# An attention and mixture-of-experts kernel: q's low halves subtracted on all 128 rows, without the two copies across partitions

## The chip, the cores and the metric

The kernel runs on one core of a Trainium2 chip. The metric is the device time of one execution in microseconds. The core has five engines with a queue each: TensorE (PE, its weight loads shown apart as PEld), VectorE (DVE), ScalarE (ACT), GpSimd (POOL) and SyncE (SP, which only issues transfers). POOL issues transfers too: the indirect ones, whose rows are picked by a table.

## What is computed

Three layers in a row, on float32 inputs:

```
scores = q @ k^T / 8                       # 4 batches x 8 heads, 768 tokens, 64 per head
keep only the first n_sink keys and a window of `window` keys behind each query
a = softmax(scores);  x = a @ v            # x: 3072 tokens x 512
h = x @ w_in;  x = (h - tanh(h)) @ w_out   # 512 -> 2048 -> 512
logits = x @ w_gate + modality_bias[modality_id];  e = argmax(logits)
out = softmax(logits)[e] * (relu(x @ w1[e]) @ w2[e])     # 8 experts, 512 -> 1024 -> 512
```

The scores decide, through everything behind them, which expert a token goes to, so most products are made from two terms: each float32 operand is split into a high half, which is the operand rounded to the type that the matmul reads (fp32r), and a low half, which is the rest.

## The kernel before

**Staging.** The 3072 tokens go through attention and the second layer in 12 chunks of 256 (index `c`). Attention works on 96 units `U`, one head of one chunk each, eight to a chunk, and runs about a chunk ahead of the second layer. In the second layer a chunk has 16 steps `f`: `L1` makes `h` (line 172), `gact` bends it on ACT, DVE and POOL, `g_split` splits the result into high and low halves (the low one on POOL, line 216), and `L2` adds it up in `acc` (line 246). After a chunk, `r_route` picks the experts of its tokens on DVE and writes a list of slots to DRAM (`xs`) with two indirect transfers from POOL (line 656). Behind the last chunks the expert layer runs, with its own lines from 712 on.

**A unit of attention.** `a_load` and `a_loadv` load q, k and v, laid out so that q and k stand twice, on rows 0 to 63 and again on rows 64 to 127 (64 is the size of a head). The first 14 units use them as they are. From unit 14 on, `a_split` makes three tiles: `K` with k's high half on the upper 64 rows and its low half on the lower 64; `A`, cast from q on all 128 rows by ACT (line 211), its lower 64 rows then overwritten by q's low half on POOL (line 216); and `B`, the same two halves the other way round, brought there by two transfers of SP (lines 301 and 302). `a_S` multiplies both with `K` (lines 314 and 315). As the contraction runs over 128 rows, A with K gives high by high and low by low, and B with K gives the two cross terms: all four products. `a_splitv` splits v in the same way (line 216 again, tile `V`). Then come the softmax, the transposes (347, 348), the band selection on POOL (355, tile `X`) and the product with v (413 to 419).

**Order.** A table of times `self.o` sets when each step is written out; the instructions then stand in that order in each engine's queue, and each engine works through its queue in order. A framework puts in the waits: each engine counts its finished instructions in a semaphore (`PE_49`, `Activation_49`, `Pool_49`, `DVE_49`), and each transfer counts its landing in one of eight semaphores for SP's transfers (`DMAHW0_49` to `DMAHW7_49`) or for POOL's (`DMASW0_49` to `DMASW7_49`). Tiles `A`, `B`, `K` and the raw `q`, `k`, `v` have two buffers each.

Of the kernel before, what the change touches and what calls it, by code (L numbers as in the profile page):

```python
# [17 lines left out]
B, H, S, D = 4, 8, 768, 64  # L18
# [18 lines left out]
def f32(ap):  # L37
    return ap.bitcast(F32)


class Kern:
# [250 lines left out]
    def a_split(self, U):  # L292
        nc = self.nc
        u, p = self.u[U], self.spp
        q, k = u.pop("q"), u.pop("k")
        A = p.tile([P, CH], F32R, tag="A", name=f"A{U}")
        Bt = p.tile([P, CH], F32R, tag="B", name=f"B{U}")
        K = p.tile([P, KW], F32R, tag="K", name=f"K{U}")
        self.cast(self.e("qhi", U < 16), A, q)
        self.sub(self.e("qlo", U < 16), A[D:], q[D:], f32(A[D:]))  # L300
        nc.sync.dma_start(f32(Bt[:D]), f32(A[D:]))
        nc.sync.dma_start(f32(Bt[D:]), f32(A[:D]))
        self.cast(self.e("khi", U < 16), K, k)
        self.sub(self.e("klo", U < 16), K[D:], k[D:], f32(K[D:]))
        u.update(A=A, B=Bt, K=K)
# [698 lines left out]
```

## Time and profile before

| | |
|---|---|
| median of 3 runs | 1222.81 us (1222.67 to 1223.86) |
| the profiled execution | 1225.8 us, of which the span from first to last instruction is 1224.0 us |
| PE busy | 1135.9 us, 93% of the span |
| DVE, ACT, POOL busy | 885.5 (72%), 757.4 (62%), 657.7 us (54%) |
| B's transfers | 164 of 64 KB (both sides counted), 2.1 us to landing |
| xs's transfers | 24, on POOL's queue, 3.8 to 7.6 us to landing, median 4.7 |

The stages, read from the trace: up to about 90 us the second layer's weights come in and are decoded; from 190 to 850 us stand the ten stretches in which a chunk's attention and second layer run side by side; from about 860 us on the expert layer runs. A busy PE doesn't say that it runs at its full clock: PEclk is the share of it that was granted, 1.00 or 0.50. An idle stretch of an engine is put down to what the engine waited for last; where several semaphores are waited for, that name can be the wrong one.

### The profile page before, as it was taken

To read this page: it belongs to the slowest core of one execution; us is meant where nothing else is said; L and a number is where in the kernel's file an instruction comes from. 1 tells how busy PE (TensorE), PEld (TensorE's weight loads), DVE (VectorE), ACT (ScalarE), POOL (GpSimd) and SP (SyncE) were. 2 spreads that over 40 slices of the span, in tenths; PEclk is the share of its full clock that TensorE was granted. 3 is DMA by queue.
4 is the path that set the end of the run, shared out by engine and by line. 5 is a ranking of instruction groups with operands and counts; after the bars stand their busy time and mean duration, and the time that the engine had idled before them with its cause. 6 is when DMAs were issued, how large, how long until landed. Compare 5 with 4: busy or idle time off the path is not lost. (4 is left out here: it accounts for less than half of the span.)

```text
span 1224.0 us, 23714 instructions
## 1 busy us (share of the span) xinstructions
PE 1135.9 (93%) x7171; PEld 994.8 (81%) x7171; DVE 885.5 (72%) x2419; ACT 757.4 (62%) x2123; POOL 657.7 (54%) x973
## 2 busy tenths in 40 slices
PE   7879998999899899999899999999798999999993
PEld 3447787988789789989789988988687989999992
DVE  6889896888778687978778887966647566666720
ACT  3445765777577678767577877775726555555620
POOL 4987865777667668767667767763302211211200
PEclk9859998999999899999999999999998999999997
DMA  7654232333323233333333323200909777777500
GB/s 206 203 187 137 75 91 62 102 80 102 60 76 90 71 88 85 98 69 104 60 91 83 104 66 87 81 12 19 343 19 327 238 226 213 222 241 219 168 26 6
DMA packets 88256, 147.98 MB, mean 121 GB/s; under 512 B 18864, under 2 KB 64432, under 8 KB 88112
## 3 DMA queue, kind: packets, MB, share of 16 engines
q1 hardware_dynamic: 83184, 133.16, 37.2%
q0 software_dynamic: 4928, 13.14, 3.0%
q8 instruction: 61, 1.00, 0.4%
q14 instruction: 83, 0.68, 0.2%
HBM read 122.86 MB, written 13.17 MB: 111 GB/s over the span
## 5 line engine op out<-in xcount | busy, mean ns | idle before, releaser
L172 PE MATMUL h<-xt,wi 128*128 128x256 f32 x2304 | 356.1, 290 | 9.9 <-DVE gz L188 9.0
L246 PE MATMUL acc<-wo,g 128*128 128x512 f32 x1152 | 334.5, 407 | 24.0 <-POOL g L216 23.1
L172 PEld LDWEIGHTS h<-xt,wi 128*128 128x128 f32 x2304 | 320.5, 194 | 40.4 <-DVE gz L188 12.4
L246 PEld LDWEIGHTS acc<-wo,g 128*128 128x128 f32 x1152 | 198.6, 192 | 53.1 <-POOL g L216 26.0
L216 POOL TENSOR_TENSOR g<-gz,g 128x256 fp32r<-128x256 f32 x192 | 153.4, 802 | 82.3 <-ACT g L211 78.4
L735 DVE TENSOR_TENSOR ml<-mr,mh 128x1024 fp32r<-128x1024 f32 x104 | 127.9, 1236 | 53.4 <-ACT mh L734 51.8
L778 PE MATMUL mh<-mxt,mh 128*128 128x256 f32 x832 | 157.9, 286 | 3.2 <-DVE mxt L768 2.5
L795 PE MATMUL macc<-mh,mg 128*128 128x512 f32 x416 | 147.9, 401 | 4.3 <-DVE mg L782 4.3
L778 PEld LDWEIGHTS mh<-mxt,mh 128*128 128x128 f32 x832 | 138.1, 193 | 12.1 <-DVE mxt L768 2.9
L189 ACT ACTIVATE u<-u,kt 128x256 f32<-128x256 f32 x192 | 97.8, 509 | 80.2 <-DVE gz L188 73.8
L355 POOL TENSOR_SCALAR_AFFINE_SELECT X<-fl 128x512 fp32r<-128x512 f32 (+1 forms) x192 | 119.2, 643 | 33.6 <-DVE fl L385 24.5
L804 POOL DMA_INDIRECT out_dram<-mo,mi x26 | 28.5, 1096 | 200.2 <-ACT mo L803 196.0
L734 ACT CAST mh<-mr 128x1024 fp32r<-128x1024 f32 x104 | 108.6, 1052 | 40.9 <-PE macc L795 25.2
L188 DVE TENSOR_TENSOR gz<-u,h 128x256 f32<-128x256 f32 x192 | 78.9, 414 | 57.5 <-POOL g L216 34.2
L778 PE MATMUL mh<-mxt,ml 128*128 128x256 f32 x416 | 118.5, 286 | 0.0
L194 DVE SCALAR_TENSOR_TENSOR gz<-gy,gz 128x256 f32<-128x256 f32 x192 | 108.3, 570 | 9.2 <-ACT gy L185 2.7
L328 ACT ACTIVATE e<-e,nm 128x160 f32<-128x160 f32 x192 | 82.0, 427 | 48.0 <-DVE nm L326 46.5
L211 ACT CAST g<-gz 128x256 fp32r<-128x256 f32 x192 | 77.0, 402 | 44.4 <-DVE gz L194 29.7
L337 POOL TENSOR_SCALAR e<-e,sm 128x160 f32<-128x160 f32 x192 | 96.9, 515 | 11.6 <-DVE sm L332 9.6
L216 POOL TENSOR_TENSOR A<-q,A 64x256 fp32r<-64x256 f32 x82 | 69.4, 846 | 56.3 <-issue 14.0
L781 ACT ACTIVATE mg<-mh 128x256 fp32r<-128x256 f32 x104 | 40.3, 387 | 94.2 <-PE mh L778 88.3
L185 ACT ACTIVATE gy<-u,k 128x256 f32<-128x256 f32 x192 | 96.5, 510 | 2.5
(211 smaller groups left out, 2270.5 us busy)
## 6 DMA issues: line engine op xcount, KB each, us to landing
mr<-in_moe_w_dram SPq DMA_DIRECT2D x104, 512.0 KB, 4.7
k<-in_k_dram SPq DMA_DIRECT2D x82, 224.0 KB, 2.7
v<-in_v_dram SPq DMA_DIRECT2D x96, 128.0 KB, 2.3
q<-in_q_dram SPq DMA_DIRECT2D x82, 128.0 KB, 2.2
B<-A SPq DMA_DIRECT2D x164, 64.0 KB, 2.1
rawi<-in_moe_w_in_dram SPq DMA_DIRECT2D x16, 512.0 KB, 5.7
rawo<-in_moe_w_out_dram SPq DMA_DIRECT2D x16, 512.0 KB, 5.6
x2d<-x SPq DMA_DIRECT2D x24, 256.0 KB, 2.2
```

The lines of the kernel that those rows point to most:

```text
L172: nc.tensor.matmul(h[:, :CH], w[:, wl, k * P:(k + 1) * P], x[:, xl, k], start=(n == 0), stop=(n == 11))
L185: nc.scalar.activation(y, u, AF.Square, bias=self.k0, scale=K1)
L189: nc.scalar.activation(u, u, AF.Relu, bias=self.kt, accum_out=self.over[:, n:n + 1])
L194: nc.vector.scalar_tensor_tensor(out=z, in0=y, scalar=KC, in1=z, op0=ALU.add, op1=ALU.mult)
L216: (self.nc.vector if eng == "v" else self.nc.gpsimd).tensor_tensor(out=out, in0=a, in1=b, op=ALU.subtract)
L246: nc.tensor.matmul(o, g[:, gl, t * P:(t + 1) * P], w[:, wl], start=(f == 0 and n == 0), stop=(f == NF - 1 and n == 2))
L337: self.nc.gpsimd.tensor_scalar(out=e, in0=e, scalar1=r, scalar2=1.0, op0=ALU.mult, op1=ALU.mult)
L355: self.nc.gpsimd.affine_select(out=out, in_=in_, pattern=[[0, n], [s, P]], base=0, channel_multiplier=-s, compare_op=ALU.is_gt if prev els ...
L734: nc.scalar.copy(hi, r)
L735: nc.vector.tensor_sub(lo, r, f32(hi))
L778: nc.tensor.matmul(h, w[:, k * P:(k + 1) * P], x[:, xl, k], start=(n == 0), stop=(n == 11))
L795: nc.tensor.matmul(self.macc[g][t], gt[:, gl, t * P:(t + 1) * P], w[:, DM:], start=(f == 0 and n == 0), stop=(f == n8 - 1 and n == 2))
```

## The change

```diff
         self.cast(self.e("qhi", U < 16), A, q)
-        self.sub(self.e("qlo", U < 16), A[D:], q[D:], f32(A[D:]))
-        nc.sync.dma_start(f32(Bt[:D]), f32(A[D:]))
-        nc.sync.dma_start(f32(Bt[D:]), f32(A[:D]))
+        self.sub(self.e("qlo", U < 16), Bt, q, f32(A))
         self.cast(self.e("khi", U < 16), K, k)
```

`A` now keeps q's high half on all 128 rows, and `B` is q's low half on all 128 rows, made on POOL from `q` and `A`. With `K` unchanged, A by K gives high by high and high by low, B by K gives low by high and low by low: the same four products, summed in another order. It touches the 82 units from 14 on. PE, DVE and ACT have the same instructions in the same order as before. POOL has the same number in the same order, with 82 of them on 128 rows instead of 64, and SP loses 164 transfers. The waits that the framework puts in are others.

On POOL, from the indirect transfers of the first chunk's routing on, before (`xs` is the list of slots, `A23` the tile A of unit 23, `V20` the split v of unit 20, `g1_7` the split of chunk 1, step 7; in brackets the semaphores waited for):

```order
L656 DMA xs_63<-pl_336,sl0_2220 4864x2 [waits DVE_49]
L656 DMA xs_63<-pl_336,sl0_2220 4864x2
L216 TENSOR_TENSOR A23_2479<-q23_2164,A23_2479 64x256 [waits DMAHW0_49,DMASW1_49,DMAHW1_49,DMASW0_49,DMAHW3_49,Activation_49,Pool_49]
L216 TENSOR_TENSOR V20_2346<-v20_2161,V20_2346 128x4x64 [waits PE_49,DMAHW4_49,Activation_49,Pool_49]
L216 TENSOR_TENSOR g1_7_2435<-gz1_7_2431,g1_7_2435 128x256 [waits Activation_49]
L355 AFFINE_SELECT X_173<-fl20_2382 128x512 [waits DVE_49]
L355 AFFINE_SELECT X_173<-fl20_2382 128x512
```

The same place on POOL now (line numbers behind the edit are two lower):

```order
L654 DMA xs_63<-pl_336,sl0_2206 4864x2 [waits DVE_49]
L654 DMA xs_63<-pl_336,sl0_2206 4864x2
L216 TENSOR_TENSOR B23_2462<-q23_2150,A23_2461 128x256 [waits DMAHW2_49,PE_49,Activation_49]
L216 TENSOR_TENSOR V20_2330<-v20_2147,V20_2330 128x4x64 [waits DMAHW4_49,PE_49,Activation_49]
L216 TENSOR_TENSOR g1_7_2417<-gz1_7_2413,g1_7_2417 128x256 [waits Activation_49]
L353 AFFINE_SELECT X_173<-fl20_2364 128x512 [waits DVE_49,Pool_49]
L353 AFFINE_SELECT X_173<-fl20_2364 128x512 [waits Pool_49]
```

No instruction moved there; the subtraction's list of waits is shorter by both DMASW semaphores, by two DMAHW ones and by POOL's own, and PE's is new in it, while the two selections now wait for POOL's own semaphore. Before, ten of the 82 subtractions wait for DMASW semaphores, one behind each of the first ten chunks' routing; now none does.

On SP, the transfers around unit 23 and 24, before:

```order
L302 DMA B23_2480<-A23_2479 64x256 [waits DMAHW2_49,DMAHW3_49,PE_49,Activation_49]
L270 DMA k25_2476<-in_k_dram 128x448 [waits DVE_49]
L269 DMA q25_2475<-in_q_dram 128x256 [waits DMAHW4_49,Pool_49]
L301 DMA B23_2480<-A23_2479 64x256 [waits DMAHW5_49]
L280 DMA v22_2472<-in_v_dram 128x256 [waits DMAHW6_49,Pool_49]
L302 DMA B24_2602<-A24_2601 64x256 [waits DMAHW0_49,DMAHW7_49,PE_49,Activation_49]
L269 DMA q26_2597<-in_q_dram 128x256 [waits Pool_49]
L270 DMA k26_2598<-in_k_dram 128x448 [waits DMAHW1_49,DVE_49]
```

And now:

```order
L270 DMA k25_2458<-in_k_dram 128x448 [waits DMAHW3_49,DVE_49]
L269 DMA q25_2457<-in_q_dram 128x256 [waits DMAHW2_49,Pool_49]
L280 DMA v22_2454<-in_v_dram 128x256 [waits DMAHW4_49,Pool_49]
L269 DMA q26_2577<-in_q_dram 128x256 [waits DMAHW6_49,Pool_49]
L270 DMA k26_2578<-in_k_dram 128x448 [waits DMAHW5_49,DVE_49]
```

The loads stand in the same order, without B's transfers between them.

## Rows read from the trace of the kernel before

**Rows 1.** The page's part 1: busy us of each engine, share of the span.
```profile
PE 1135.9 (93%) x7171; PEld 994.8 (81%) x7171; DVE 885.5 (72%) x2419; ACT 757.4 (62%) x2123; POOL 657.7 (54%) x973
```

**Rows 2.** PE's waits from 190 to 850 us: total us, times, longest us.
```profile
PE acc L246 <- POOL g L216: 22.4, 8, 5.6
PE R L413 <- POOL V L216: 4.6, 2, 2.3
```

**Rows 3.** PE's timeline, 194 to 210 us: start, us, instructions [idle before, releaser].
```profile
195.19 0.99 PE L172 MATMUL h<-xt,wi 128*128 128x256 f32 x7
201.75 1.22 PE L246 MATMUL acc<-wo,g 128*128 128x512 f32 x2 [5.56 <-POOL g L216]
```

**Rows 4.** POOL's timeline over the same place, 189 to 203 us.
```profile
192.25 0.98 POOL L656 DMA_INDIRECT xs<-pl,sl  x1 [0.30 <-issue]
199.49 0.72 POOL L216 TENSOR_TENSOR A<-q,A 64x256 fp32r<-64x256 f32 x1 [6.26 <-DMA k<-in_k_dram]
200.29 0.72 POOL L216 TENSOR_TENSOR V<-v,V 128x256 fp32r<-128x256 f32 x1
200.97 0.72 POOL L216 TENSOR_TENSOR g<-gz,g 128x256 fp32r<-128x256 f32 x1
```

**Rows 5.** Transfers issued from 192 to 200 us: count, KB, us to landing.
```profile
xs<-pl,sl POOLq DMA_INDIRECT x1, 6.9
```

**Rows 6.** POOL's timeline behind the next chunk's routing, 262 to 270 us.
```profile
264.24 0.97 POOL L656 DMA_INDIRECT xs<-pl,sl  x1 [0.30 <-issue]
265.22 0.74 POOL L216 TENSOR_TENSOR g<-gz,g 128x256 fp32r<-128x256 f32 x1
```

**Rows 7.** POOL's waits from 190 to 850 us, those before A's subtraction.
```profile
POOL A L216 <- issue: 12.9, 2, 6.8
POOL A L216 <- DMA k<-in_k_dram: 12.2, 2, 6.3
...
POOL A L216 <- DMA B<-A: 8.5, 2, 4.3
POOL A L216 <- PE s L315: 2.9, 1, 2.9
```

**Rows 8.** From one routing's transfer to the next: length, busy us (instructions) of PE, PEld, DVE, ACT, POOL, PEclk, DMA share, GB/s.
```profile
190.72:262.84 72.12, 66.24 (x443) 60.55 (x442) 56.10 (x175) 49.07 (x161) 46.22 (x75) 0.95 0.33 83
...
323.04:394.39 71.35, 65.18 (x434) 59.28 (x433) 52.92 (x175) 47.49 (x154) 44.96 (x73) 0.95 0.32 78
394.39:467.10 72.71, 67.43 (x447) 61.26 (x447) 54.69 (x174) 49.82 (x162) 47.40 (x76) 0.95 0.31 78
467.10:527.92 60.82, 60.54 (x424) 55.79 (x423) 51.87 (x167) 46.47 (x152) 46.63 (x73) 1.00 0.33 91
527.92:594.35 66.43, 63.64 (x430) 58.05 (x430) 54.02 (x176) 47.17 (x155) 45.82 (x73) 0.97 0.33 85
594.35:665.75 71.40, 66.29 (x447) 60.33 (x447) 54.67 (x174) 49.75 (x162) 47.64 (x76) 0.98 0.33 80
665.75:726.62 60.87, 60.56 (x425) 55.80 (x423) 51.85 (x167) 46.47 (x152) 46.69 (x73) 1.00 0.33 91
726.62:792.74 66.12, 63.38 (x430) 57.76 (x429) 54.30 (x176) 47.13 (x155) 46.14 (x74) 0.97 0.31 79
```

**Rows 9.** The six stretches from 190 to 850 us with PEclk 0.50: the first, and their sum.
```profile
200.16:206.98 6.82, 5.24 (x19) 4.85 (x20) 3.92 (x10) 3.21 (x11) 6.06 (x11) 0.50 0.20 54
...
sum 30.68, PE 26.59 PEld 23.74 DVE 21.84 ACT 16.63 POOL 28.03; mean PE 4.43 PEld 3.96 DVE 3.64 ACT 2.77 POOL 4.67
```

**Rows 10.** POOL's instructions from 190 to 850 us by shape: busy us, mean ns, idle before.
```profile
L216 POOL TENSOR_TENSOR A<-q,A 64x256 fp32r<-64x256 f32 x73 | 62.0, 849 | 53.4 <-issue 12.9 <-DMA k<-in_k_dram 12.2 <-ACT A L211 9.2
L216 POOL TENSOR_TENSOR V<-v,V 128x256 fp32r<-128x256 f32 x76 | 58.1, 764 | 27.6 <-ACT V L211 23.6 <-PE T L348 1.9 <-DMA B<-A 0.2
```

**Rows 11.** SP's waits from 190 to 850 us, the longest in total.
```profile
SPq L302 <- PE s L315: 189.5, 64, 5.2
```

**Rows 12.** The stretch before the first routing, columns as in rows 8.
```profile
90.00:190.72 100.72, 96.43 (x586) 79.37 (x586) 91.46 (x233) 66.11 (x206) 73.86 (x103) 0.98 0.33 98
```

## The prediction

> **What bounds the kernel now.** I read the page first: PE is busy for 93% of the span [rows 1], so time can only be won where PE stands still or runs at half its clock. PE's waits come next, in the stage that the change touches. From 190 to 850 us PE waits ten times, 22.4 + 4.6 = 27.0 us in all, for POOL: for the low half of g at line 246, and twice for V [rows 2]. They are the two longest entries of that view, and no row of it names B's transfers, so B never comes too late for PE, and what the diff seems to offer (two transfers of 2 us less on the way to the scores) is worth nothing by itself.
>
> The third view is the timeline at the longest of these waits. PE ends its last matmuls at 196.2 us (195.19 + 0.99) and starts again at 201.75 [rows 3]. POOL, which it waits for, issues the second of the routing's two indirect transfers at 192.25, and then does nothing until 199.49, when A's subtraction starts; V's and g's subtractions follow, g's at 200.97 to 201.69, and PE goes on 0.06 us later [rows 4]. What does POOL wait for? The profile names the load of k, but the subtraction doesn't read k. The order of before gives the subtraction's list of waits, and two DMASW semaphores stand in it: it waits until the routing's own transfers have landed. This second one landed 6.9 us after its issue [rows 5], at 199.15; the subtraction starts 0.3 us behind that. The same list stands at ten subtractions, one behind each of the first ten routings.
>
> The ten are an experiment that the kernel makes by itself. Behind the second routing the order has two subtractions of g, two selections and a sum on POOL before the subtraction of A comes: POOL goes on with g at 265.22, 0.01 us behind the second transfer's end [rows 6], and A has that much work ahead of it to wait behind. In seven of the ten A comes sooner, and POOL idles before it: 12.9 + 12.2 + 8.5 + 2.9 = 36.5 us under four different names, seven times [rows 7].
>
> Cut the stage at the routings and the cost stands out [rows 8]. Where the wait costs nothing a chunk takes 60.82 and 60.87 us, with PE idle for 0.3 us and PEclk 1.00. The six stretches with a long wait take 66.1 to 72.7 us, with PEclk 0.95 to 0.98: each such wait of PE is followed by a stretch at the lower of its two clock levels, 1.2 instead of 2.4 GHz, six stretches in all, 30.68 us, in which PE was busy for 26.59 [rows 9].
>
> **The change part by part.**
>
> Gone: the wait for the landing. The list of B's subtraction has no DMASW any more. That it is not merely written elsewhere: the only waits of POOL on DMASW that the changed kernel adds in this stage stand at the next routing's transfers, for the landing of the one before, a chunk (60 to 73 us) earlier, so they cost nothing. Two sums for what comes back. Directly: 27.0 us of PE's waits, and half of the 26.59 us in which it worked at half clock, 13.3, together 40.3 us. By rate: the two clear stretches take 121.69 us for 424 + 425 = 849 matmuls, 0.1433 us each; the six others hold 443 + 434 + 447 + 430 + 447 + 430 = 2631, which at that rate are 377.1 us, and they took 420.13: 43.0 us. The first counts a few tenths that have other reasons, the second leaves out the seventh wait (2.9 us on POOL [rows 7], less on PE). I take 42.
>
> Gone: 164 transfers on SP. SP spent 189.5 us of this stage waiting at line 302 for B's buffer [rows 11], with the loads of q, k and v queued behind. They will be issued earlier, up to the buffer that each of them waits for itself. Nobody on PE's path waits for these loads, so it is worth 0. At most it gives what PE idles from 90 to 190 us, where the first of these transfers stand among the last weights: 100.72 - 96.43 = 4.3 us [rows 12].
>
> Changed: 82 subtractions on 128 rows instead of 64. Of the two nearest rows one is A's own, 849 ns on 64 rows, the other V's, the same operation on 128 rows with as many elements in each row, 764 ns [rows 10]. I take no difference: 82 x (764 - 849) would be -7 us of POOL, which isn't the bound. The other end, that rows cost in proportion, is the rival below.
>
> Added: PE in the subtraction's list, for B's buffer. ACT's cast of A, which the subtraction waits for, already waits for the matmul just before that one in PE's queue (A and B of a unit are used back to back), so the new wait is over before the old one: 0. Behind it on POOL stand V and g, and it would be PE that waits for them. Added too: waits for POOL's own semaphore at the selections and at e's scaling (line 337). The gap that such a wait leaves between two instructions is bounded by V behind A, where V has one now: 199.49 + 0.72 to V's start, less than 0.1 us [rows 4]; by the order of both kernels some 160 come, at the selections and at e, and some 150 go, at A, V and g, so about 1 us of POOL, which isn't the bound. So 0.
>
> Next late: with POOL in time, PE at its full rate, as in the clear stretches. The expert layer behind 860 us has the same instructions in the same order; it starts earlier and is as long.
>
> The sum against the profiled execution: 1225.8 - 42 = 1183.8 us. The median of the runs shown is 3.0 us below that execution, so the forecast is 1222.8 - 42 = 1181 us.
>
> **The rivals.**
>
> DVE takes over. In a clear stretch it is busy 51.87 of 60.82 us, 85.3%; at the rate of 0.1433 us the six would have it at up to 56.10 of 63.5, 88%. If 85.3% were the most that it can reach, the six stretches with their 56.10 + 52.92 + 54.69 + 54.02 + 54.67 + 54.30 = 326.70 us of DVE would take 326.70 / 0.853 = 383.0 us, and 37 us come back instead of 43: 1186. For it: DVE and POOL hand each other gz and g. Against it: PE idles 0.3 us at 85%, which is no sign of an edge.
>
> Part of the wait comes back. POOL is still in order, and something else (the cast of A late on ACT, gz late on DVE while the routing's small instructions run) could hold the subtraction before g. If half returns, the time is 1222.8 - 21 = 1202. For it: PE's waits after a stall are only seen as they are, with everything behind the stall shifted. Against it: the clear stretches have the same routing and the same casts, and no such wait.
>
> POOL isn't waiting but working. The row of an indirect transfer is 1 us, and if POOL went on for 6 us behind it, unseen, no semaphore would matter and the time would stay at 1223. Rows 6 speak against it: g's subtraction runs 0.01 us behind the second transfer, while that is still in flight. This is where the Trainium skill has a rule against the change: its page Perfetto Trace Analysis, section DMA Instruction — SWDGE (GPSIMD), has the descriptors written by two of GpSimd's processors and ends the shown interval when the last is written, and the section on GpSimd's instructions calls its intervals unreliable. By that rule the idle 6 us could be work, and the change worth nothing; the trace does not bear it out here.
>
> Slower: the 128 rows cost double. Then each of 82 subtractions adds 0.85 us to POOL, eight to a chunk, 6.8 us on the 46.6 us that it is busy in a clear stretch of 60.8 [rows 8]. It decides from the point where POOL's chain from gz to g has no slack left; if PE waits for all of it, 82 x 0.85 = 70 us come on top and 42 go: 1251. Against it: V's 764 ns on 128 rows [rows 10].
>
> **How the numbers follow.** The forecast, all seven waits gone and nothing in their place, has 0.74; its own range is 1173 to 1192. The low end is all of the rate's 43.0, the 2.9 of the seventh wait and the 4.3 of rows 12, 50 us; the high end has PE's waits back and the lower clock at a third of its 13.3, 31 us. DVE as the bound has 0.10 and lies within. Half coming back has 0.07, no change 0.04, slower 0.04, and 0.01 is for more than I can add up. The range of 1172 to 1200 holds the first two and part of the third. A measurement of this kernel tells 0.2%, 2.4 us, from no change: faster 0.92, same 0.04, slower 0.04.
>
> **What would show it.** In the changed kernel's trace POOL goes from the routing's second transfer to its next instruction within a microsecond in all ten chunks; the rows "POOL B" have no wait of several us; PE's waits for POOL g and V from 190 to 850 us fall from 27 to below 5 us; PEclk shows 1.00 from 100 us to the expert layer; each stretch between routings takes 60 to 65 us; B's subtraction takes 0.72 to 0.85 us. I am wrong if POOL still idles behind line 654, if PE's waits turn up under another name in the same places, or if the subtraction's mean rises above 1 us.

## The result, and the profile after

The changed kernel takes 1184.46 us (median of four runs, 1182.99 to 1186.29), the kernel before, timed beside it, 1223.34 us: a ratio of 0.968, 95% interval 0.966 to 0.970, 38.9 us less. The profiled execution of the changed kernel took 1182.99 us, with a span of 1181.3. Line numbers behind the edit are two lower than before: the routing's transfers stand at line 654, the scores' matmuls at 312 and 313, e's scaling at 335.

The page's busy us by engine, to be held against [rows 1], and the granted clock of TensorE in 40 slices of the span:

```profile
PE 1120.0 (95%) x7171; PEld 984.2 (83%) x7171; DVE 887.1 (75%) x2419; ACT 755.3 (64%) x2123; POOL 662.2 (56%) x973
...
PEclk9999999999999999999999999999999999999996
```

POOL's count is the same and its busy time 4.5 us more; PE's busy time fell by 15.9 us for the same 7171 matmuls. PE's waits from 190 to 850 us (total us, times, longest), where [rows 2] had 22.4 and 4.6 us for POOL g and POOL V:

```profile
PE h L172 <- DVE gz L188: 3.5, 4, 1.8
PE mh L776 <- DVE mxt L766: 2.3, 1, 2.3
PE s L312 <- DVE nm L324: 1.7, 6, 0.7
PE T L345 <- POOL e L335: 1.3, 5, 0.4
...
PE acc L246 <- POOL g L216: 0.3, 1, 0.3
```

The wait for g is 0.3 us, that for V is gone. The next in line is gz on DVE with 3.5 us. POOL's timeline at the first routing, the place of [rows 4] (start, us, instruction, idle before):

```profile
190.95 0.98 POOL L654 DMA_INDIRECT xs<-pl,sl  x1 [0.31 <-PE h L172]
191.94 0.77 POOL L216 TENSOR_TENSOR B<-q,A 128x256 fp32r<-128x256 f32 x1
192.63 0.77 POOL L216 TENSOR_TENSOR V<-v,V 128x256 fp32r<-128x256 f32 x1
193.33 0.76 POOL L216 TENSOR_TENSOR g<-gz,g 128x256 fp32r<-128x256 f32 x1
```

Where 6.26 us of nothing stood between the transfer's issue and the subtraction, there is 0.01 us, although this transfer takes longer to land than the one in [rows 5]; the transfers issued at that place, with us to landing:

```profile
xs<-pl,sl POOLq DMA_INDIRECT x1, 7.5
```

By the shown interval of 0.98 us the transfer's issue was over at 191.93. The Trainium skill's page Perfetto Trace Analysis, section DMA Instruction — SWDGE (GPSIMD), ends that interval when the descriptors are written, not when the data has moved; this trace agrees, since three subtractions run to 194.09 while the data is in flight until 198.45.

The stretches from one routing to the next, with the columns of [rows 8]:

```profile
189.45:252.67 63.22, 63.02 (x443) 58.22 (x442) 56.20 (x175) 48.74 (x161) 47.60 (x75) 1.00 0.32 78
252.67:312.94 60.27, 58.53 (x402) 53.12 (x401) 51.62 (x166) 44.55 (x145) 44.84 (x73) 1.00 0.24 70
312.94:376.38 63.44, 62.47 (x434) 57.09 (x434) 54.71 (x175) 47.31 (x154) 45.72 (x74) 1.00 0.30 72
376.38:441.36 64.98, 64.30 (x446) 58.82 (x446) 53.29 (x173) 49.22 (x161) 48.08 (x77) 1.00 0.28 70
441.36:502.55 61.19, 60.94 (x428) 56.31 (x427) 52.22 (x168) 47.08 (x152) 45.79 (x73) 1.00 0.27 74
502.55:564.32 61.77, 61.41 (x427) 56.10 (x427) 54.64 (x176) 46.95 (x155) 46.74 (x73) 1.00 0.28 74
564.32:629.30 64.98, 64.30 (x446) 58.81 (x446) 53.35 (x173) 49.33 (x161) 48.14 (x77) 1.00 0.30 70
629.30:691.00 61.70, 61.26 (x430) 56.64 (x429) 52.30 (x168) 47.24 (x152) 45.80 (x74) 1.00 0.26 74
691.00:752.77 61.77, 61.25 (x425) 55.80 (x425) 54.60 (x176) 46.97 (x155) 46.70 (x74) 1.00 0.26 68
752.77:808.03 55.26, 55.10 (x378) 50.24 (x378) 34.29 (x117) 37.57 (x115) 26.41 (x41) 1.00 0.05 15
```

PEclk is 1.00 in all ten. The six stretches that [rows 8] shows at 0.95 to 0.98 took 420.13 us and take 380.16; the two clear ones, 60.82 and 60.87, take 61.19 and 61.70. The sums of the same view over the ten, before and then after:

```profile
sum 658.90, PE 626.92 PEld 572.16 DVE 515.94 ACT 465.75 POOL 442.59; mean PE 62.69 PEld 57.22 DVE 51.59 ACT 46.58 POOL 44.26
```

```profile
sum 618.58, PE 612.58 PEld 561.13 DVE 517.23 ACT 464.96 POOL 445.83; mean PE 61.26 PEld 56.11 DVE 51.72 ACT 46.50 POOL 44.58
```

That is the whole result in two rows: the ten stretches are 40.32 us shorter; for 25.98 us of these PE had stood idle (658.90 - 626.92 against 618.58 - 612.58), and for 14.34 us it had been busy longer with the same matmuls. Of the 14.34, half of the 26.59 us that [rows 9] shows at the lower clock gives 13.3; the other 1.0 us has no row of its own.

### The profile page after: what moved, and what is told of

It reads as the page before. It is cut to its first block, busy times and chain, and to the rows that moved or that the text cites. A ratio compares the mean times of both kernels' runs of the same rounds, so it can differ in the third digit from the quotient of the medians.

```text
span 1181.3 us, 23220 instructions
## 1 busy us (share of the span) xinstructions
PE 1120.0 (95%) x7171; PEld 984.2 (83%) x7171; DVE 887.1 (75%) x2419; ACT 755.3 (64%) x2123; POOL 662.2 (56%) x973
## 5 line engine op out<-in xcount | busy, mean ns | idle before, releaser
L246 PE MATMUL acc<-wo,g 128*128 128x512 f32 x1152 | 328.0, 401 | 2.2 <-ACT g L211 1.4
L246 PEld LDWEIGHTS acc<-wo,g 128*128 128x128 f32 x1152 | 195.8, 189 | 28.9 <-ACT g L211 2.2
L211 ACT CAST g<-gz 128x256 fp32r<-128x256 f32 x192 | 76.7, 400 | 36.5 <-DVE gz L194 27.5
L793 PEld LDWEIGHTS macc<-mh,mg 128*128 128x128 f32 x416 | 77.8, 190 | 17.4 <-DVE mg L780 4.6
```

Source lines behind the costliest of these rows:

```text
L246: nc.tensor.matmul(o, g[:, gl, t * P:(t + 1) * P], w[:, wl], start=(f == 0 and n == 0), stop=(f == NF - 1 and n == 2))
L793: nc.tensor.matmul(self.macc[g][t], gt[:, gl, t * P:(t + 1) * P], w[:, DM:], start=(f == 0 and n == 0), stop=(f == n8 - 1 and n == 2))
```

## The experiments

The theory: POOL's subtraction of A waited until the routing's transfers had landed, and that wait cost PE 27 us of standing still and a lower clock behind it. The wait stands in the program's lists, and there it belongs to a subtraction on POOL that starts at row 64. The edit takes away two things at once, that start and the copies, and the prediction did not say which of them takes the wait out of the list. The rivals: the two copies through SP cost the time, or the work on 64 rows or in place does. All experiments ran on chips on which the kernel before took 1216 to 1218 us; each is judged by the kernel before that ran beside it. The changed kernel itself was timed again beside two of them, the tiny instruction from row 0 and the subtraction on DVE.

**The copies away, the start at row 64 kept.** From the kernel before:

```
-        Bt = p.tile([P, CH], F32R, tag="B", name=f"B{U}")
-        nc.sync.dma_start(f32(Bt[:D]), f32(A[D:]))
-        nc.sync.dma_start(f32(Bt[D:]), f32(A[:D]))
-        u.update(A=A, B=Bt, K=K)
+        u.update(A=A, B=A, K=K)
```

> The kernel before with its subtraction kept in place on A's lower 64 rows, and without the two transfers and without B: the second product reads A again, so the two cross terms are left out of the scores. Theory (the wait for the routing's transfers at a subtraction that starts at row 64 is the whole cost, the copies cost nothing): nine or ten subtractions still wait for DMASW semaphores, five of them (behind routings 0, 2, 3, 5 and 6) within two POOL instructions of the transfers. The stretches behind these stay at 66 to 72 us, POOL waits before A add up to some 30 us, and the time is 1210 to 1224 us. Rival (the 164 transfers on SP and the waits on them are the cost): 1180 to 1190 us, no waits of several us on POOL.

Measured: 1220.68 us, ratio 1.0025 (1.0009 to 1.0042). Without a single copy nothing is won. The time alone doesn't settle it, since PE's order is another one here (the seventh stretch has 487 matmuls and takes 77.41 us, above the 72 expected, and the eighth 384 and 57.54); the waits do. PE's waits and one of POOL's in this kernel's trace, 190 to 850 us:

```profile
PE acc L246 <- POOL g L216: 14.5, 5, 5.8
PE R L410 <- POOL V L216: 7.6, 3, 5.2
```

```profile
POOL A L216 <- DMA xs<-pl,sl: 27.0, 5, 6.4
```

PE's two waits are still 22.1 us. And this profile calls POOL's wait by its name: in [rows 7] it stood under issue, k's load, B's copies and a matmul; here it is the routing's transfer xs, five times, 6.4 us at the longest.

**The change, and the copies put back to no purpose.** To the changed kernel:

```
+        Ct = p.tile([P, CH], F32R, tag="C", name=f"C{U}")
+        nc.sync.dma_start(f32(Ct[:D]), f32(Bt[D:]))
+        nc.sync.dma_start(f32(Ct[D:]), f32(A[:D]))
```

> The changed kernel with two transfers of the old size added per unit, into a spare tile that nothing reads (B's rows 64 on to rows 0 to 63, A's first 64 rows to rows 64 on). Theory: the transfers stand on SP and on the DMA queues as before the change, but the subtraction starts at row 0 and waits for no DMASW semaphore: 1182 to 1189 us, PE's waits for POOL from 190 to 810 us below 3 us. Rival (transfers are the cost): 1215 to 1225 us.

Measured: 1183.44 us, ratio 0.9726 (0.9698 to 0.9753). All engines but SP have the changed kernel's instructions in the same order, and the 164 transfers cost nothing that can be told from no change. With the experiment ahead of it: not the copies.

**The kernel before, with its subtraction on the other 64 rows.** One line; all copies, the 64 rows and the work in place stay:

```
-        self.sub(self.e("qlo", U < 16), A[D:], q[D:], f32(A[D:]))
+        self.sub(self.e("qlo", U < 16), A[:D], q[:D], f32(A[:D]))
```

> The kernel before with one difference: the in-place subtraction is done on rows 0 to 63 of A instead of rows 64 to 127 (q stands on both, and B is copied from A by the same two transfers, so the four products are the same). Theory: with a start at row 0 no DMASW semaphore is waited for, so this brings the whole gain with 64 rows and all 164 transfers: 1182 to 1190 us. Rival (transfers): 1215 to 1225 us. Rival (128 rows against 64 matters): the subtraction's mean would differ from the changed kernel's by more than 100 ns; the theory has it within 50 ns.

Measured: 1186.03 us, ratio 0.9745 (0.9718 to 0.9772). That is nearly the whole gain (the changed kernel beside its own runs of before: 0.9736, 0.9709 to 0.9762), out of D: turned into :D. PE has the same matmuls in the same order in the kernel before, the changed one and this one, so they can be held against each other stretch by stretch (here the ten sum to 620.68 us). PE's wait for g and POOL's row for the subtraction in this trace:

```profile
PE acc L246 <- POOL g L216: 0.6, 2, 0.3
```

```profile
L216 POOL TENSOR_TENSOR A<-q,A 64x256 fp32r<-64x256 f32 x73 | 62.2, 852 | 8.6 <-ACT A L211 7.6 <-PE h L172 0.5
```

The idle time before it is 8.6 us, nearly all for the cast, where [rows 10] has 53.4. Its 852 ns are 11 ns from the changed kernel's 863 on 128 rows, so the rival of the rows falls, too.

**The change, and a tiny instruction that starts at row 64.** One column in each of the 82 units, and behind it the same on the rows from 0, as a control:

```
+        tn = p.tile([P, 1], F32, tag="tn", name=f"tn{U}")
+        nc.gpsimd.tensor_tensor(out=tn[D:], in0=q[D:, :1], in1=f32(A[D:, :1]), op=ALU.subtract)
```

> The changed kernel with one POOL instruction added behind each of the 82 subtractions: one column of 64 rows from row 64 on, into a tile that nothing reads. Its list of waits has DMASW semaphores nine times, 2, 10, 2, 3, 10, 9, 5, 2, 10 and 3 POOL instructions behind the transfers of routings 0 to 9 (the sixth and seventh waits stand at places where POOL has other work). Theory: the wait alone brings the cost back, and where it stands decides: the stretches behind routings 0, 2, 3, 7 and 9 get 4 to 9 us longer than in the changed kernel, those behind 1, 4, 5 and 8 stay within 1.5 us, and the time is 1205 to 1225 us, without any copy. Rival (copies, SP): 1184 to 1192 us, the 82 added instructions being 0.2 us each on POOL, which isn't the bound.

Measured: 1215.98 us, ratio 0.9986 (0.9969 to 1.0003): one column on 64 rows gives all of the gain back.

```
-        nc.gpsimd.tensor_tensor(out=tn[D:], in0=q[D:, :1], in1=f32(A[D:, :1]), op=ALU.subtract)
+        nc.gpsimd.tensor_tensor(out=tn[:D], in0=q[:D, :1], in1=f32(A[:D, :1]), op=ALU.subtract)
```

> The changed kernel with one tiny POOL subtraction more in each of the 82 units, one column of q on rows 0 to 63. It is the control for e4_tiny_row64, where the same instruction stands at the same place of POOL's queue but on rows 64 to 127; the order of POOL is the same in both, and only there does it wait for the routing's landing. If what costs time is that wait, which goes with a start at row 64: 1184 to 1192 us (the bare change, plus up to the 309 ns that each of these instructions took in e4, 25 us of POOL, which is not the bound), no wait of several us before tn, and PE's waits for POOL g below 2 us from 190 to 815 us. If e4 lost its 32 us because one more instruction on POOL delays g, wherever it stands: again 1212 to 1218 us.

Measured: 1199.75 us, ratio 0.9866 (0.9841 to 0.9890). The two kernels have the same instructions in the same order on all five engines. What differs stands in the lists of waits; unit 23's on POOL, the first behind a routing, from row 64 and then from row 0:

```
L302 TENSOR_TENSOR tn23_2484<-q23_2164,A23_2479 64x1 [waits DMASW1_49,DMASW0_49,Pool_49]
L302 TENSOR_TENSOR tn23_2484<-q23_2164,A23_2479 64x1
```

Ten of the 82 have DMASW in their lists in the first kernel (its expectation says nine, but counts out ten places), none in the second. POOL's rows for tn, first from row 64 (a wait from 190 to 840 us, and the group: busy us, mean ns, idle before), then from row 0:

```profile
POOL tn L302 <- DMA xs<-pl,sl: 17.6, 6, 5.0
```

```profile
L302 POOL TENSOR_TENSOR tn<-q,A 64x1 f32<-64x1 f32 x73 | 22.5, 309 | 22.8 <-DMA xs<-pl,sl 17.6
```

```profile
L302 POOL TENSOR_TENSOR tn<-q,A 64x1 f32<-64x1 f32 x73 | 28.0, 384 | 0.0
```

So the landing's wait is worth 0.9986 - 0.9866 = 0.012, 14.6 us (some 11 to 18 by the two intervals; the two kernels ran on different chips, each beside its own kernel before), and in the two profiled executions 18.6 us over the ten stretches (651.98 against 633.33 in the sums below). It lies where the wait follows closely on the transfers, in the stretches behind the first, third, fourth and eighth routing. From row 64, with the columns of [rows 8], and then from row 0:

```profile
189.88:260.26 70.38, 65.64 (x437) 59.92 (x436) 55.09 (x174) 48.31 (x159) 49.45 (x84) 0.95 0.26 67
321.11:389.64 68.53, 64.87 (x431) 59.02 (x431) 51.12 (x173) 47.40 (x155) 46.78 (x81) 0.95 0.26 66
389.64:460.11 70.47, 69.16 (x479) 63.33 (x478) 54.89 (x179) 53.23 (x170) 50.91 (x86) 1.00 0.26 69
655.40:723.69 68.29, 64.11 (x430) 58.20 (x429) 53.61 (x172) 47.74 (x154) 49.60 (x84) 0.98 0.23 69
```

```profile
192.39:255.42 63.03, 62.73 (x436) 57.55 (x435) 55.95 (x174) 47.99 (x158) 49.18 (x85) 1.00 0.29 74
316.18:379.77 63.59, 62.73 (x434) 57.20 (x434) 52.62 (x173) 47.44 (x155) 47.68 (x81) 1.00 0.28 72
379.77:448.02 68.25, 68.20 (x473) 62.53 (x472) 56.19 (x178) 52.90 (x168) 51.27 (x86) 1.00 0.27 70
642.45:707.07 64.62, 62.76 (x429) 56.80 (x428) 52.73 (x172) 47.37 (x154) 51.09 (x84) 1.00 0.25 73
```

These four are 7.4, 4.9, 2.2 and 3.7 us longer from row 64, 18.2 us of the 18.6. The rest, up to the change's 1185, is a miss of both expectations: I had the tiny instruction at 0 to 8 us, and its 0.2 us on POOL came from no row; it took 309 and 384 ns. Its sums, from row 64, from row 0, and of the changed kernel's run beside the latter:

```profile
sum 651.98, PE 628.80 PEld 570.46 DVE 509.88 ACT 469.65 POOL 458.70; mean PE 62.88 PEld 57.05 DVE 50.99 ACT 46.97 POOL 45.87
```

```profile
sum 633.33, PE 621.25 PEld 564.19 DVE 519.12 ACT 469.98 POOL 462.18; mean PE 62.13 PEld 56.42 DVE 51.91 ACT 47.00 POOL 46.22
```

```profile
sum 619.11, PE 612.85 PEld 561.21 DVE 517.86 ACT 465.30 POOL 445.86; mean PE 61.28 PEld 56.12 DVE 51.79 ACT 46.53 POOL 44.59
```

The tiny instruction costs 14.2 us where nothing waits for a landing: PE is idle for 12.1 us instead of 6.3, and busy for 8.4 us more. With the added instruction PE's order is another one than the changed kernel's, and POOL has 28 us more work; how the 14 us divide between the two stays open. The run from row 64 left its expectation in four stretches: against the changed kernel the fifth is 3.3 us longer, the sixth 7.6, the tenth 3.2, and the ninth 2.1 shorter. That is not the wait: from row 0, without it, the fifth and sixth take 64.56 and 69.19 us beside 64.51 and 69.32, and the other two are within 1.3 us of each other.

**The kernel before, with the subtraction on DVE.** Copies, 64 rows and the start at row 64 all stay; the table has qlo='v' instead of 'g', which moves all 82 subtractions (the expectation says from the sixteenth unit on).

> The kernel before, with copies, 64 rows and the start at row 64 all kept, but A's subtraction on DVE for the units from the sixteenth on (before: on POOL). DVE issues no transfers, and its subtraction has no wait for the routing's landing. If the cost lies in POOL's wait for that landing: 1180 to 1200 us; the middle is the change's 1184, and the high end has DVE, 52 us busy in a clear stretch of 61, with six to eight more subtractions of about 0.4 us in each, 3 us in each of ten stretches, at most half of it in PE's way. If the copies, or the start at row 64 on whatever engine, are what costs: 1215 to 1230 us, with PE's waits for POOL g at 20 us or more from 190 to 850 us.

Measured: 1189.57 us, ratio 0.9774 (0.9752 to 0.9796). On DVE, which has no transfer of its own in flight, the start at row 64 brings no such wait. PE's wait for g from 190 to 835 us, and DVE's row for the subtraction:

```profile
PE acc L246 <- POOL g L216: 3.6, 2, 2.4
```

```profile
L216 DVE TENSOR_TENSOR A<-q,A 64x256 fp32r<-64x256 f32 x73 | 36.7, 503 | 3.2 <-ACT A L211 1.4
```

The 4 us by which it is behind the changed kernel come with another order of PE's and with 16 us more of DVE's busy time (902.4 against 886.5 on the pages of the two); no experiment parts these.

**The change and the kernel before, once more.**

> The change as it is, timed on the same chip as its neighbours here, as the yardstick for them. 1181 to 1187 us, 0.966 to 0.974 of the kernel before.

Measured: 1185.13 us, ratio 0.9736 (0.9709 to 0.9762). The changed kernel's time is the same to 0.7 us, and yet the gain is 31 us instead of 39, since the kernel before takes 1216 on these chips. So I ran that one for its trace, twice.

> The kernel before, word for word, to have its trace from the chips on which the other experiments ran: there it took 1211 to 1220 us, beside 1223 to 1225 where the change was first timed, and the change gave 31 us instead of 39. Expected: 1211 to 1222 us and a ratio within 0.003 of 1. If the wait for the landing costs less there because the routing's second transfer lands sooner, its landings are shorter than the 4 to 7.6 us of the first trace, by half a microsecond or more on average, and PE's waits for POOL g and V come to 22 us or less from 190 to 850 us. If the waits are the same and only the clock answers them in another way, they stay at 25 to 29 us and the half-clock stretches in the ten chunks come to less than 30.7 us: 7 us less of them explain some 3.5.

> The same again, for a second trace: how much the landings, PE's waits and the half-clock stretches differ from one execution to the next. As e8_before; if the difference between chips is noise of single executions, the two differ from each other by as much as from the first trace.

Measured: 1215.43 us, ratio 1.000 (0.998 to 1.002), and 1216.96, ratio 1.000 (0.998 to 1.002). PE's waits and POOL's before A in the first of the two, to be held against [rows 2] and [rows 7]:

```profile
PE acc L246 <- POOL g L216: 18.0, 8, 5.0
PE R L413 <- POOL V L216: 3.1, 2, 1.9
```

```profile
POOL A L216 <- DMA k<-in_k_dram: 15.9, 3, 5.7
...
POOL A L216 <- DMA B<-A: 7.8, 3, 3.9
POOL A L216 <- issue: 5.1, 1, 5.1
...
POOL A L216 <- ACT g L211: 2.5, 1, 2.5
```

PE waits 21.1 us instead of 27.0, POOL 31.3 instead of 36.5. In the second the numbers are 22.0 and 31.5. These two traces show a landing for every other routing's second transfer. That of the first, third, fifth, seventh and ninth lands after 6.9, 7.4, 6.0, 7.1 and 5.9 us in the trace of [rows 5], after 6.3, 5.8, 5.5, 6.2 and 5.6 in the first of these, and after 6.2, 6.3, 5.7, 6.3 and 5.5 in the second: means of 6.7, 5.9 and 6.0, so the two later executions are nearer to each other than to the first. The half-clock stretches in the ten come to 27.3 and 23.9 us instead of 30.7. The ten stretches in the first of the two:

```profile
sum 652.00, PE 625.94 PEld 571.46 DVE 515.82 ACT 464.20 POOL 442.62; mean PE 62.59 PEld 57.15 DVE 51.58 ACT 46.42 POOL 44.26
```

652.00 instead of 658.90, and 651.94 in the second, so 6.9 us of the 9.5 and 10.2 us between the spans (1224.0, 1214.5, 1213.8) lie there. The landing's part of the expectation holds, and the clock's comes with it: 5.9 and 5.0 us less waiting, and 1.0 and 1.8 us less by the clock (half of what PE's busy time at half clock fell by, from 26.6 to 24.5 and 23.1 us), in sum 6.9 and 6.8 of the 6.9 and 7.0. The kernel before passes on how long a transfer takes to land; the changed one doesn't: at the same five places its two traces have means of 6.9 and 6.2 us, and its time is the same. Why it lands sooner on these chips was not tried.

**What stays open of the cause.** Shown is which instruction gets the wait (POOL, two inputs, a start at row 64: the kernel before, the first and the fourth experiment) and which doesn't (a start at row 0, or DVE). Why it is given is not: the subtraction reads and writes nothing that the routing's transfers touch, and neither does tn. Whether it takes two inputs, and whether another start than row 64 brings it as well, no run tried. Along with DMASW the list names POOL's own semaphore; by these names the instruction is held until what POOL has begun is done, its transfers included. The Trainium skill's page GPSIMD Engine Reference, section Instruction dispatch, asks for a wait on POOL's own earlier instruction where one reads partitions that another of its eight cores wrote; no run here shows whether the wait stems from that rule, and it asks for none on a transfer. Taking the wait alone away was not tried.

## Why the prediction was right, step by step

Forecast were 1181 us in a range of 1172 to 1200; it is 1184.5, and faster.

- **The place and the cause** were right: ten subtractions waiting for a landing, seven of them in PE's way. What in the edit takes the wait out was not forecast; the runs show it. Moving the start row alone does it, the copies alone don't, and the tiny instruction brings it back.
- **What comes back**: the direct sum, 27.0 of waits and 13.3 of clock, 40.3, is what the ten stretches gave, 26.0 and 14.3, 40.3. That it agrees to a tenth is in part luck: its two terms miss by 1.0 us each, in opposite directions. The sum by rate, 43.0, was too high by 3.0: the six stretches take 380.16 us where 0.1433 us for each matmul had made 377.1. It took PE's idle time in a clear stretch, 0.3 us, for that of all, and the six keep 3.4 us of it (380.16 less 376.75 busy); and it priced matmuls of 128 to 512 columns alike in stretches with different shares of them. I took 42, nearer to the wrong one: this is the term that was mis-sized.
- **Against the profiled execution**: 1225.8 - 40.3 = 1185.5, and the changed kernel's was 1183.0. The other 2.4 us of the spans' difference lie ahead of the ten (1.3) and behind them (1.1). Outside the ten before's traces also differ among themselves: the two later ones are shorter there by 2.6 and 3.2 us. The forecast took its 42 from the median, 3.0 us lower; with 40.3 it would have been 1182.5.
- **The 164 transfers**, at nothing, at most 4.3 us: right, by the spare copies. SP's wait for B's buffer [rows 11] went over to the load of q, which now waits for POOL's B; SP's longest wait from 190 to 850 us:

```profile
SPq L269 <- POOL B L216: 205.1, 61, 6.5
```

  It is a longer total than before, and PE has no wait for any load.
- **128 rows**, at no difference: right. POOL's group, to be held against [rows 10]:

```profile
L216 POOL TENSOR_TENSOR B<-q,A 128x256 fp32r<-128x256 f32 x73 | 63.0, 863 | 10.7 <-ACT A L211 9.8 <-PE h L172 0.6
```

  863 ns on 128 rows, 849 and 852 on 64. The 764 ns of V, which I had named as the other end, was not what B would take; 0.85 as the upper bound of what I would see missed by 0.01 us. The rival that rows double the cost falls.
- **The new wait for PE** shows as 0.6 us before B at most, and POOL's waits for itself as 0.3 us before X: at nothing, right.
- **The rivals.** DVE as the bound falls: it is busy 56.20 of 63.22 us, 89%, in the first stretch, above the 85.3% that would have been its most. PE's longest wait is for DVE now, but 3.5 us in 660. Half of the wait coming back falls: 0.3 us for g. That POOL works behind the transfer falls: B starts 0.01 us behind it.
- **What was to be seen** was seen but for two edges: POOL goes on within a microsecond, PE's clock is 1.00 from 100 us to the tenth stretch's end, and of the ten stretches nine lie between 60 and 65 us. The eleventh stretch, on the way to the expert layer, has a clock of 0.97, and the tenth has less to do, 55.26 us (56.88 before).

What the runs added is that the gain has no fixed size: 38.9 us beside a kernel before of 1223, 31.3 beside one of 1216. The range was wide enough for either, but for a reason it did not name.

## What to carry to other kernels

When an engine idles behind its own transfers, read the wait list of the instruction that starts late, not the name that the profile gives the wait: here it stood under four names, none of them the transfer's. Then ask what in the instruction brings that wait into the list, since it may be as little as the row at which a tile begins, and try that alone before taking away what looks expensive. Where PE's waits and its lower clock come in pairs, add up both from their own rows, the waits and half of the busy time at half clock. That sum gave 40.3 us where 40.3 came back, and from the two later traces of the kernel before some 33.4 and 33.5 where its ten stretches are 32.9 and 32.8 us longer than the changed kernel's 619.11; a rate taken from the clear stretches was 3 us too high.

## What the runs showed of the hardware

- A small indirect transfer's landing is long and not steady: 3.6 to 8.8 us in the traces of the kernel before and the changed one, the longest of them in the changed kernel, where no subtraction waits for it. All of one stage's together move 0.02 MB. The Trainium skill's page DMA: Bandwidth & Descriptors, section Anatomy of one DMA — SWDGE (gpsimd) path, has a fixed 2.0 us and the bytes over 436 GB/s; the traces here show 1.8 to 4.4 times that from issue to landing.
- POOL's subtraction with 256 elements in a row took about as long on 64 rows (849 and 852 ns) as on 128 (863). With one element in a row it still took 309 to 384 ns on 64 rows.
- PE's waits cost more than their length: with 26 us of idle time went 14 us by which its matmuls had taken longer, most of it in six stretches at the lower of the two clock levels.
